# Attention with forget decay and a gated FFN on one core: last tokens' units earlier, turns of the second batch moved, PSUM slots of a pair swapped

**Chip, cores, metric.** One core of one Trainium2 chip. Times are device microseconds (us) of that core; quoted times are medians over runs. Every run named here was correct, and every profiled run was fast, with a granted TensorE clock of 0.998 to 1.000.

## The reference, cut

```python
# q, k, v: (B=8, H=8, S=576, D=64); f: (8, 8, 576); all float32
scores = scale * np.matmul(q, k.transpose(0, 1, 3, 2))
cum    = np.cumsum(np.log(np.clip(f, 0.0001, 1.0)), axis=-1)
scores = np.where(causal, -1e9, scores + cum[..., :, None] - cum[..., None, :])
attn   = softmax(scores)                       # cut
x      = (attn @ v).transpose(0, 2, 1, 3).reshape(4608, 512)
gate   = 1.0 / (1.0 + np.exp(-(x @ w_gate)))   # w_gate, w_val: (512, 1536)
out    = (gate * (x @ w_val)) @ w_out          # w_out: (1536, 512)
```

The output has 4608 tokens of 512 values in float32.

## The kernel before

The kernel interleaves two things on TensorE. The FFN runs in chunks of 512 tokens ("c0", "c1", ...), each of 36 steps; the step numbers below count through the chunks (step 46 is step 10 of c1). The attention of the batches that come later is put between the steps as small pieces of work. All 5259 matmuls of the trace write one PSUM tile, `ps`, which the kernel lays out as eight banks of 512 float32 per partition: banks 4 to 7 belong to the FFN, banks 0 and 1 are attention's slot 0, banks 2 and 3 its slot 1.

```python
def T_step(p, bank, copy_q, copy_k):        # a "turn": q and k of a head pair, transposed
    if bank < 4:
        slot_free(bank // 2)
    ...
    banks = [psh[:, 1024 * x:1024 * x + S] for x in (bank, bank + 1)]
    for t in range(TPP):
        for half, bank in zip((LO, HI), banks):
            for h in range(2):
                nc.tensor.transpose(...)    # 36 small transposes
    qT, kT = pair_T(p)
    for dst, bank, copy in ((qT, banks[0], copy_q), (kT, banks[1], copy_k)):
        copy(...)                           # on ScalarE (ACTC) or VectorE (DVEC)

def slot_free(slot):                        # let the chain run on until it lets go of the slot
    while chain and slot in chain_holds[0]:
        pop_chain()

def S_unit(p, u, slot, tag=None):           # a score unit: C, A, B, D (or Z: the last tokens)
    slot_free(slot)
    sc = 2 * slot
    ...                                     # matmuls of two heads into banks sc and sc + 1
    nc.scalar.activation(e[:, :, 0:w], ps[:, sc:sc + 2, 0:w], ACTF.Exp, scale=scale)
    ...                                     # causal mask on GpSimd

def out_two(p, now):                        # two pairs: sums, values, then a chain of VectorE work
    while chain:
        pop_chain()
    ...                                     # 120 matmuls; the values of pair p end in banks 2 and 3
    def last():                             # the last readers of banks 2 and 3
        for x, k, y in ((0, 2, 0), (0, 2, 1), (1, 1, 1)):
            part(x, k, y)                   # -> scaled(): tensor_tensor on VectorE, line 271
        cross_x(p, 2)
    both, beta = {0, 1}, {1}
    chain_holds[0] = both
    chain.extend([(flip, both), (lambda: spr(1), both), (lambda: part(1, 1, 0), beta),
                  (lambda: spr(0), beta), (last, set())])
    pop_chain(now)

def rest_turn():                            # last 64 tokens of batch 0, transposed into xR
    slot_free(1)
    ...                                     # 16 transposes of xt into banks 3 and 2 (line 435)
    ...                                     # 2 copies on ScalarE, 2 on VectorE (line 440)
```

The schedule of the second batch (batch 1), in c0, and of batches 2 and 3:

```python
for x, (w, bank, copy) in enumerate(((4, 0, DVEC), (4, 2, DVEC), (22, 0, ACTC), (24, 2, DVEC))):
    put(w, lambda p=P + x, bank=bank, copy=copy: T_step(p, bank, ACTC, copy))
for w, x, tag in ((7, 0, "D"), (9, 1, "A"), (11, 2, "B")):
    put(w, lambda p=x + 1, tag=tag: S_unit(p, "Z", 1, tag))
put(12, rest_values)
put(17, rest_turn)
batch(1, (6, 8, 10, 12, 13, 14, 15, 16, 24, 25, 26, 26, 27, 27, 28, 29), (18, 30),   # outs at 18, 30
      (0, 0, 0, 0, 1, 0, 1, 0, 0, 0, 1, 0, 1, 0, 1, 0))                             # slots
...
for b, ts in ((2, (36, 37, 39, 44)), (3, (67, 69, 71, 76))):
    for x, t in enumerate(ts):
        put(t, lambda b=b, x=x: T_step(b * P + x, (0, 2, 2, 2)[x], DVEC if x > 1 else ACTC, DVEC))
batch(2, (38, 40, 42, 43, 46, 47, 48, 49, 55, 57, 58, 59, 60, 61, 62, 62), (52, 64))
batch(3, (70, 72, 74, 75, 78, 79, 80, 81, 87, 89, 91, 92, 94, 95, 97, 98), (84, 100))
```

The softmax here doesn't subtract the row's maximum and nothing guards it: scores larger than these inputs give would overflow.

Of the kernel before, what the change touches and what calls it, by code (L numbers as in the profile page):

```python
# [15 lines left out]
def kernel(  # L16
# [12 lines left out]
    B, H, S, D = q.shape  # L29
# [142 lines left out]
    def pair_T(p):  # L172
        b, a = divmod(p, HPAIR)
        return qTs[b % 2][:, a, :], kTs[b % 2][:, a * SPAD:(a + 1) * SPAD]


    def k_at(p, jt):
        b, a = divmod(p, HPAIR)
        o = a * SPAD + jt * NP if b < 4 else (jt * HPAIR + a) * NP
        return kTs[b % 2][:, o:o + NP]  # L180
# [5 lines left out]
    def T_step(p, bank, copy_q, copy_k):  # L186
        if bank < 4:
            slot_free(bank // 2)
        b, hf, ho = half_of(p)
        src = qktiles[b, hf]  # L190
# [4 lines that stand above are left out]
                    nc.tensor.transpose(  # L195
                        bank[64 * h:64 * h + 64, t * QP:(t + 1) * QP],
                        src[half, ho + h, t * D:(t + 1) * D], ident_bf[half, half])
        qT, kT = pair_T(p)
        for dst, bank, copy in ((qT, banks[0], copy_q), (kT, banks[1], copy_k)):
            copy(dst[:, 0:S].rearrange("p (n t) -> p n t", t=TPP),  # L200
                 bank.rearrange("p (t n) -> p n t", t=TPP))
# [27 lines left out]
    def slot_free(slot):  # L229
        while chain and slot in chain_holds[0]:  # L230
            pop_chain()

    def S_unit(p, u, slot, tag=None):
        slot_free(slot)
        sc = 2 * slot
        qT = pair_T(p)[0]
        pieces, w, diag = UNITS[u]
        for jt, i0, i1, c in pieces:
            for h in range(2):
                hp = slice(64 * h, 64 * h + 64)  # L240
                nc.tensor.matmul(ps[:, sc + h, c:c + i1 - i0],  # L241
                                 k_at(p, jt)[hp, :], qT[hp, i0:i1],
                                 start=True, stop=True)
        tag = tag or TAGS.get(u, u)
        e = st[p, u] = esb.tile([128, 2, WIDE[tag]], BF16, tag="e" + tag, name="e" + tag)
        nc.scalar.activation(e[:, :, 0:w], ps[:, sc:sc + 2, 0:w], ACTF.Exp, scale=scale)  # L246
        m, pat = diag(e)
        nc.gpsimd.affine_select(out=m, in_=m, compare_op=ALU.is_ge, fill=0.0,  # L248
                                base=0, pattern=pat, channel_multiplier=-1)

    def vg_step(p, eng=None):
        b, a = divmod(p, HPAIR)
        vg = asb.tile([128, NJT, 2, D + 2], BF16, tag="vg", name="vg")
        st[p, "vg"] = vg
        if p < HPAIR:
            (eng or nc.gpsimd).tensor_copy(vg[:, :, :, D], g_bf[:, :, 2 * p:2 * p + 2])
        (eng or nc.gpsimd).tensor_tensor(  # L257
            out=vg[:, :, :, 0:D], in0=vbs[b % 2][:, :, 2 * a:2 * a + 2, :],
            in1=g_bf[:, :, 2 * p:2 * p + 2].unsqueeze(3).to_broadcast([128, NJT, 2, D]),
            op=ALU.mult)  # L260
# [111 lines left out]
    def out_two(p, now):  # L372
        while chain:
            pop_chain()
        Z = norm_tile("Z", [128, S])
        r = norm_tile("r", [128, 2, NB])
        R = norm_tile("R", [128, 2, S])
        for i, hi, o in main_tail(0):
            sums_two(p, o, i, hi)
        sums_of(Z, main_tail(0))  # L380
        for y in range(2):
            for x in (1, 0):
                i, hi, o = main_tail(2 - x)[y]
                vals_two(p + x, o, i, hi)

        def flip():
            inverse(r[:, 0, :], Z)
            nc.vector.tensor_copy(r[:, 1, :], r[:, 0, :])

        def spr(x):  # L390
            to_pair(r, x)
            spread(R[:, x, :], r[:, x, :])

        def part(x, k, y):
            i, hi, o = main_tail(k)[y]
            scaled(p + x, o, R[:, x, :], i, hi)

        def last():
            for x, k, y in ((0, 2, 0), (0, 2, 1), (1, 1, 1)):
                part(x, k, y)  # L400
# [7 lines that stand above are left out]
# [136 lines left out]
    DVEC, ACTC = nc.vector.tensor_copy, nc.scalar.copy  # L544
    T_step(0, 4, ACTC, DVEC)
    gps = ps[:, 7, 0:NJT * BH].rearrange("p (t n) -> p t n", t=NJT)
    for t in range(NJT):
        w = NP if t < NJT - 1 else TAIL
# [46 lines left out]
    def put(s, fn):  # L595
        at.setdefault(s, []).append(fn)

    def batch(b, units, outs, slots=(0, 0, 1, 0, 1, 0, 1, 0)):
        P = b * HPAIR
        for n, s in enumerate(units):  # L600
            p, u = P + n // 4, "CABD"[n % 4]

            def unit(p=p, u=u, n=n):
                S_unit(p, u, slots[n % len(slots)])
                if u == "C" and p not in late_vg:
                    vg_step(p)

            put(s, unit)
        for n, s in enumerate(outs):
            put(s, lambda n=n, now=3 if s % 36 < 2 * NFT else 4: out_two(P + 2 * n, now))  # L610
# [12 lines left out]
        return units, outs  # L623

    P = HPAIR
    for x, (w, bank, copy) in enumerate(((4, 0, DVEC), (4, 2, DVEC), (22, 0, ACTC), (24, 2, DVEC))):
        put(w, lambda p=P + x, bank=bank, copy=copy: T_step(p, bank, ACTC, copy))
    for w, x, tag in ((7, 0, "D"), (9, 1, "A"), (11, 2, "B")):
        put(w, lambda p=x + 1, tag=tag: S_unit(p, "Z", 1, tag))
    put(12, rest_values)  # L630
    put(17, rest_turn)
    batch(1, (6, 8, 10, 12, 13, 14, 15, 16, 24, 25, 26, 26, 27, 27, 28, 29), (18, 30),
          (0, 0, 0, 0, 1, 0, 1, 0, 0, 0, 1, 0, 1, 0, 1, 0))
    for p, w in zip(late_vg, (13, 15)):
# [9 lines left out]
    for b, ts in ((2, (36, 37, 39, 44)), (3, (67, 69, 71, 76))):  # L644
        for x, t in enumerate(ts):
            put(t, lambda b=b, x=x: T_step(b * P + x, (0, 2, 2, 2)[x], DVEC if x > 1 else ACTC, DVEC))
    batch(2, (38, 40, 42, 43, 46, 47, 48, 49, 55, 57, 58, 59, 60, 61, 62, 62), (52, 64))
    batch(3, (70, 72, 74, 75, 78, 79, 80, 81, 87, 89, 91, 92, 94, 95, 97, 98), (84, 100))
    o, G = 100, 99
    for b in range(4, B):  # L650
        units, outs = later(o, G)
# [59 lines left out]
```

## Time and profile before

| what | value |
|---|---|
| time | 376.23 us, median of 3 runs (375.75 to 376.54) |
| span in the profiled run | 375.7 us |
| TensorE busy | 96% of the span, and 91% of the chain that ended last |
| largest wait of TensorE after the first loads | 1.1 us (at 11.7 us, a score unit for a copy on ScalarE); past 28 us, where the change lies, 0.4 us apart from the stops named below |

The profiled run itself took 377.45 us, 1.2 us above the median. Single runs of one kernel differ by about 1 us here. There were also three stops of TensorE of which the profile can name no releaser ("issue"):

```profile
PE ps L352 <- issue: 0.8, 1, 0.8
```

(List of waits of TensorE, kernel before: line waited at, then us in total, times, longest us. This one is at 256.9 us; the second is at 222.6 us.) The third lies in the stretch that the change touches. In the chain of waits (start, length) it is the last line here, in the FFN work behind the 120 matmuls of `out_two` at step 18:

```profile
45.56 2.21 PE ps L352 x120
47.77 0.97 PE ps L455 x7
48.74 0.09 issue
```

### The profile page before, as it was taken

Reading aid. Unit: us, or ns where it says so; the run is one execution under the profiler, and the core shown is the slowest. Engines: PE = TensorE matmul, PEld = TensorE weight load, DVE = VectorE, ACT = ScalarE, POOL = GpSimd, SP = SyncE. Lnnn points to the kernel's source line nnn. Section 1 sums busy time; section 2 is a strip of 40 time slices with the busy share of each in tenths; the row PEclk is TensorE's granted clock in tenths of the full one; section 3 lists DMA queues with packets and bytes.
Section 4 is the critical chain, followed back from the end, with each engine's and each line's share of the span. In section 5 each row is a group of like instructions: output and inputs, shape, how many; then the busy total and the mean of one; then the engine's idle time right before and its main releaser. Section 6 shows DMA issues by size and latency. Waiting matters only on the chain.

```text
span 375.7 us, 12208 instructions
## 1 busy us (share of the span) xinstructions
PE 360.1 (96%) x5259; PEld 193.7 (52%) x5264; DVE 177.5 (47%) x382; ACT 196.4 (52%) x294; POOL 168.1 (45%) x265
## 2 busy tenths in 40 slices
PE   2889999999999999999999999999999999999996
PEld 1547544456655645454675545544456544444442
DVE  5874481566475565274708370747055713312320
ACT  5868745564836472847374727481647314323321
POOL 8896835064836664559665937460415000000000
PEclk9999999999999999999999999999999999999999
DMA  8999999599898986799984996687313131011002
GB/s 156 232 206 249 198 185 219 157 203 173 133 181 213 114 110 67 159 163 155 146 181 106 182 179 127 156 135 102 103 58 75 31 101 58 3 56 58 0 21 92
DMA packets 101349, 49.24 MB, mean 131 GB/s; under 512 B 72000, under 2 KB 94400, under 8 KB 101296
## 3 DMA queue, kind: packets, MB, share of 16 engines
q0 software_dynamic: 48704, 20.65, 44.1%
q1 hardware_dynamic: 52448, 27.68, 30.5%
q8 instruction: 41, 0.67, 0.8%
q10 hardware_dynamic: 144, 0.13, 0.1%
q14 instruction: 12, 0.10, 0.1%
HBM read 37.90 MB, written 9.44 MB: 126 GB/s over the span
## 4 chain that ended last, share of the span: by engine, by line
PE 91%; ACT 2%; DVE 2%; issue 2%; DMA 1%; POOL 1%; ACTq 0%; POOLq 0%
PE ps L455 49%; PE ps L495 17%; PE ps L352 8%; PE ps L504 8%; PE ps L241 6%; PE ps L300 1%; PE ps L195 1%; DMA qk_in<-in_k_dram 1%; DVE gv L465 1%; ACT eC L246 1%; DVE kT L200 1%; ACT eB L246 0%; DVE qT L200 0%; ACT sg L464 0%; POOL vg L257 0%
## 5 line engine op out<-in xcount | busy, mean ns | idle before, releaser
L455 PE MATMUL ps<-xR,w 64*128 64x512 bf16 x1728 | 205.7, 376 | 0.2
L465 DVE SCALAR_TENSOR_TENSOR gv<-sg,ps 128x512 bf16<-128x512 bf16 x108 | 74.0, 686 | 154.3 <-ACT sg L464 149.9
L455 PEld LDWEIGHTS <-w 64*128 64x128 bf16 x1728 | 88.6, 94 | 83.3 <-issue 3.6
L464 ACT ACTIVATE sg<-ps 128x512 bf16<-128x512 f32 x108 | 64.5, 598 | 86.9 <-PE ps L455 84.8
L248 POOL TENSOR_SCALAR_AFFINE_SELECT eC<-eC 128x256 bf16<-128x256 bf16 x32 | 13.0, 407 | 91.0 <-ACT eC L246 90.8
L241 PE MATMUL ps<-qT,kT 64*128 64x320 bf16 (+6 forms) x416 | 49.9, 275 | 2.9 <-ACT kT L200 1.3
L246 ACT ACTIVATE eC<-ps 128x896 bf16<-128x896 f32 (+1 forms) x32 | 28.1, 878 | 21.0 <-PE ps L241 21.0
L257 POOL TENSOR_TENSOR vg<-vb,g_bf 128x640 bf16<-128x640 f32 x30 | 37.9, 1263 | 0.0
L241 PEld LDWEIGHTS <-kT 64*128 64x128 bf16 x416 | 24.1, 96 | 23.7 <-issue 5.8
L482 ACT ACTIVATE ob<-ps 128x512 f32<-128x512 f32 x35 | 19.6, 596 | 32.1 <-PE ps L504 20.2
L495 PE MATMUL ps<-wox,gvx 64*128 64x512 bf16 x288 | 35.5, 376 | 0.0
L246 ACT ACTIVATE eA<-ps 128x896 bf16<-128x896 f32 (+2 forms) x33 | 30.4, 924 | 9.4 <-PE ps L241 8.7
L495 PE MATMUL ps<-wo,gv 64*128 64x512 bf16 x288 | 34.7, 376 | 0.4 <-issue 0.4
L504 PE MATMUL ps<-wo,gv 128*128 128x512 bf16 x140 | 32.3, 380 | 0.3 <-issue 0.2
L246 ACT ACTIVATE eB<-ps 128x768 bf16<-128x768 f32 (+2 forms) x33 | 27.5, 833 | 8.8 <-PE ps L241 7.4
L271 DVE TENSOR_TENSOR xR<-ps,R 128x64 bf16<-128x64 f32 (+2 forms) x68 | 26.2, 428 | 2.1
L108 POOL DMA_DIRECT2D vb<-in_v_dram x30 | 25.2, 849 | 0.2 <-issue 0.2
L263 DVE STREAM_TRANSPOSE R<-r 128x576 f32<-128x576 f32 (+1 forms) x32 | 24.6, 770 | 1.1
L495 PEld LDWEIGHTS <-gv 64*128 64x128 bf16 x288 | 15.4, 94 | 14.5 <-issue 1.3
L246 ACT ACTIVATE eD<-ps 128x640 bf16<-128x640 f32 x30 | 21.0, 701 | 3.0 <-PE ps L241 3.0
L495 PEld LDWEIGHTS <-gvx 64*128 64x128 bf16 x288 | 15.3, 94 | 13.2
L504 PEld LDWEIGHTS <-gv 128*128 128x128 bf16 x144 | 13.4, 98 | 16.8 <-issue 1.6
(82 smaller groups left out, 325.1 us busy)
## 6 DMA issues: line engine op xcount, KB each, us to landing
out_dram<-ob SPq DMA_DIRECT2D x35, 256.0 KB, 2.2
vb<-in_v_dram POOLq DMA_DIRECT2D x20, 256.0 KB, 5.4
xR<-xR SPq DMA_DIRECT2D x20, 144.0 KB, 3.4
gvx<-gv SPq DMA_DIRECT2D x12, 192.0 KB, 4.3
vb<-in_v_dram SPq DMA_DIRECT2D x8, 256.0 KB, 4.6
k_rows<-in_k_dram POOLq DMA_DIRECT2D x16, 128.0 KB, 6.8
q_rows<-in_q_dram POOLq DMA_DIRECT2D x16, 128.0 KB, 5.1
qk_in<-in_q_dram POOLq DMA_DIRECT2D x7, 288.0 KB, 6.7
```

The lines of the kernel that those rows point to most:

```text
L108: eng.dma_start(vbs[b % 2][0:n, t, h0:h1, :], rows)
L241: nc.tensor.matmul(ps[:, sc + h, c:c + i1 - i0], k_at(p, jt)[hp, :], qT[hp, i0:i1], start=True, stop=True)
L246: nc.scalar.activation(e[:, :, 0:w], ps[:, sc:sc + 2, 0:w], ACTF.Exp, scale=scale)
L257: (eng or nc.gpsimd).tensor_tensor(out=vg[:, :, :, 0:D], in0=vbs[b % 2][:, :, 2 * a:2 * a + 2, :], in1=g_bf[:, :, 2 * p:2 * p + 2].unsquee ...
L263: nc.vector.transpose(R.rearrange("p (n c) -> p n c", c=32), r.unsqueeze(2).to_broadcast([128, r.shape[1], 32]))
L271: nc.vector.tensor_tensor(out=xR[:, a, r0:r0 + n], in0=psf[:, o + i:o + i + n], in1=R[:, i:i + n], op=ALU.mult)
L352: nc.tensor.matmul(psf[32 * qd:32 * qd + 32, o + a:o + z], lhsT_of(jt, qd), e_of(u, qd)[:, c:c + z - a], start=(y == 0), stop=(y == len(to ...
L455: nc.tensor.matmul(ps[:, bk, :], w1[half, head, ft * NP:(ft + 1) * NP], xR[half, sl, t0:t0 + TCH], start=(first and x == 0), stop=(last an ...
L464: nc.scalar.activation(sg, ps[:, fb, :], ACTF.Tanh, scale=0.5)
L465: nc.vector.scalar_tensor_tensor(out=gv[:, ft, :], in0=sg, scalar=1.0, in1=ps[:, fb + 1, :], op0=ALU.add, op1=ALU.mult)
L495: nc.tensor.matmul(ps[:, bk, :], lhsT, rhs, start=(x == 0 and ft == 0), stop=(x == 1 and ft == NFT - 1))
L504: nc.tensor.matmul(ps[:, 4 + tt, :], gv[:, ft, tt * NP:(tt + 1) * NP], wo[:, ft, :], start=(ft == 0), stop=(ft == NFT - 1))
```

## The change

The intent is to fill TensorE's waits better. The units of the last tokens (Z) come three steps sooner so that their product needn't wait; the second turn of batch 1 leaves step 4, the third leaves step 22 for 17, takes slot 1 in place of slot 0 and has its k copy on VectorE, and the last tokens' turn (`rest_turn`) goes from 17 to 23. In batches 2 and 3 the second head pair takes its slots in the other order, and two units of batch 2 come a step later. (Some unchanged lines are left out of the diff.)

```diff
@@ -623,12 +623,12 @@
     P = HPAIR
-    for x, (w, bank, copy) in enumerate(((4, 0, DVEC), (4, 2, DVEC), (22, 0, ACTC), (24, 2, DVEC))):
+    for w, x, tag in ((4, 0, "D"), (6, 1, "A"), (8, 2, "B")):
+        put(w, lambda p=x + 1, tag=tag: S_unit(p, "Z", 1, tag))
+    for x, (w, bank, copy) in enumerate(((4, 0, DVEC), (10, 2, DVEC), (17, 2, DVEC), (24, 2, DVEC))):
         put(w, lambda p=P + x, bank=bank, copy=copy: T_step(p, bank, ACTC, copy))
-    for w, x, tag in ((7, 0, "D"), (9, 1, "A"), (11, 2, "B")):
-        put(w, lambda p=x + 1, tag=tag: S_unit(p, "Z", 1, tag))
     put(12, rest_values)
-    put(17, rest_turn)
+    put(23, rest_turn)
     batch(1, (6, 8, 10, 12, 13, 14, 15, 16, 24, 25, 26, 26, 27, 27, 28, 29), (18, 30),
           (0, 0, 0, 0, 1, 0, 1, 0, 0, 0, 1, 0, 1, 0, 1, 0))
@@ -644,8 +644,9 @@
-    batch(2, (38, 40, 42, 43, 46, 47, 48, 49, 55, 57, 58, 59, 60, 61, 62, 62), (52, 64))
-    batch(3, (70, 72, 74, 75, 78, 79, 80, 81, 87, 89, 91, 92, 94, 95, 97, 98), (84, 100))
+    MIXED = (0, 0, 1, 0, 0, 1, 0, 1, 0, 0, 1, 0, 1, 0, 1, 0)
+    batch(2, (38, 40, 42, 43, 46, 47, 48, 49, 55, 57, 59, 60, 60, 61, 62, 62), (52, 64), MIXED)
+    batch(3, (70, 72, 74, 75, 78, 79, 80, 81, 87, 89, 91, 92, 94, 95, 97, 98), (84, 100), MIXED)
```

## The prediction

> **What bounds the kernel now.** I read the page first, then the list of who TensorE waits for, then the chain of waits and the timelines of the steps that the change touches.
>
> ```profile
> span 375.7 us, 12208 instructions
> PE 360.1 (96%) x5259; PEld 193.7 (52%) x5264; DVE 177.5 (47%) x382; ACT 196.4 (52%) x294; POOL 168.1 (45%) x265
> PE 91%; ACT 2%; DVE 2%; issue 2%; DMA 1%; POOL 1%; ACTq 0%; POOLq 0%
> ```
>
> TensorE is busy for 96% of the span, and the chain that ended last is 91% TensorE. The change removes no matmul, copy or transfer: it moves work between steps and swaps PSUM slots. It can win only TensorE's stalls, and only those in the steps it touches (28 to 145 us). Matmul ends are modelled and hide short stalls, so I took start-to-start distances: a pair of 64-row, 512-column matmuls follows the last after 0.216 us, and what exceeds such a value is a stall. The real stalls in that stretch, in us: 0.28 at 30.12, 0.15 to 0.24 at 38.16, 0.11 at 40.03, 0.26 at 48.83, 0.56 at 56.14, 0.3 at 59.3, 0.33 at 65.5, 0.46 at 82.53, 0.31 to 0.44 at 96.57, 0.14 at 101.26, 0.45 at 121.20: about 3.5 us, 0.9% of the time. That is the ceiling of any gain, and already below 2%.
>
> The largest that the change aims at are the two waits of the score unit C for a copy on VectorE, in batches 2 and 3. In the list of TensorE's waits and then in the chain (start, length):
>
> ```profile
> PE ps L241 <- DVE kT L200: 0.6, 2, 0.3
> ...
> 78.90 0.88 PE ps L455 x8
> ...
> 79.83 0.61 ACT sg L464
> ...
> 80.46 0.69 DVE gv L465
> 81.14 0.67 DVE qT L200
> 81.81 0.67 DVE kT L200
> ...
> 82.53 0.35 PE ps L241
> ```
>
> At step 44 a turn of q and k (T_step) writes PSUM banks 2 and 3. VectorE has to do its gate product first, then both copies, until 82.48. The C unit of step 46 has slot 1, the same banks 2 and 3: its first matmul starts at 81.87, its second only at 82.53. A view of waits shows 0.3 of it; from starts, the step's FFN matmuls begin at 82.53 where 82.06 would do.
>
> [...]
>
> **The change, part by part.**
>
> *Slots in batches 2 and 3.* The second pair's C, A, B, D go from slots 1, 0, 1, 0 to 0, 1, 0, 1. C of step 46 then needs only slot 0, whose last reader, the exp of D at step 43, ended at 79.7. A of step 47 takes slot 1; it would start at 82.06 + 0.86 = 82.92, after the copies end at 82.48. B needs the exp of C as before, D that of A as before. So 82.53 - 82.06 = 0.47 us goes. In batch 3 (C of step 78) the FFN step starts at 121.21 where 120.77 would do: 0.44 us. Sum: **-0.91 us**. Both lie on TensorE's path, and nothing behind them has slack to swallow it except as below.
>
> *B and D of batch 2 one step later (58 to 59, 59 to 60).* B at 96.57 waits for the last normalisation, which reads banks 2 and 3 and ends at 96.5. A step later it finds them free: 0.3 to 0.4 us less there. But look at ScalarE:
>
> ```profile
> 97.24 0.81 ACT L246 ACTIVATE eB<-ps 128x768 bf16<-128x768 f32 x1
> 98.25 0.70 ACT L246 ACTIVATE eD<-ps 128x640 bf16<-128x640 f32 x1 [0.20 <-PE ps L241]
> 98.99 0.60 ACT L464 ACTIVATE sg<-ps 128x512 bf16<-128x512 f32 x1
> 99.49 0.91 ACT L246 ACTIVATE eC<-ps 128x896 bf16<-128x896 f32 x1
> 100.29 0.92 ACT L246 ACTIVATE eA<-ps 128x896 bf16<-128x896 f32 x1
> 101.34 0.81 ACT L246 ACTIVATE eB<-ps 128x768 bf16<-128x768 f32 x1
> 102.04 0.70 ACT L246 ACTIVATE eD<-ps 128x640 bf16<-128x640 f32 x1
> ```
>
> From the exp of B to that of the last D these seven take 0.81+0.70+0.60+0.91+0.92+0.81+0.70 = 5.45 of the 5.50 us between 97.24 and 102.74. ScalarE is full, and B's exp would start at 96.25 + 0.86 + 0.2 = 97.3, no sooner than now. TensorE saves at 58 and then waits at 61 (A for the exp of D, estimate 0.27) and 62 (D for the exp of A, 0.45). Net **-0.05 us**.
>
> *The first batch's last tokens (Z) from steps 7, 9, 11 to 4, 6, 8; the second turn of batch 1 from 4 to 10.*
>
> ```profile
> 28.87 0.83 PE L195 MATMUL ps<-ident_bf,qk_in 64*64 64x64 bf16 x72
> 29.39 1.28 DVE L465 SCALAR_TENSOR_TENSOR gv<-sg,ps 128x512 bf16<-128x512 bf16 x2 [2.58 <-PE ps L195]
> 29.63 0.89 PE L455 MATMUL ps<-xR,w 64*128 64x512 bf16 x3
> ...
> 38.16 0.51 PE L417 MATMUL ps<-vg,eD 128*64 128x65 bf16 x20
> ...
> 39.56 0.42 DVE L425 TENSOR_TENSOR gvx<-ps,r 128x256 bf16<-128x256 f32 x1
> ...
> 40.03 0.37 PE L241 MATMUL ps<-qT,kT 64*128 64x448 bf16 x2
> ```
>
> Two turns now fill 28.87 to 29.63; the FFN's second matmul then stands until 30.125 for the first gate product of VectorE, which ends at 30.08. One turn was thus free: it lay in time that TensorE had to wait anyway. With one Z unit (0.15 us) and one turn (0.38), TensorE comes to the same wait at 29.40 and waits longer. The turn that is now at step 10 costs its 0.41 us in full, the Z unit no longer at 7 gives 0.15 back: **+0.26 us**.
> What Z wins: the product of the last tokens with the values (38.16) waits some 0.24 us for the exp of the third Z, and that goes. But C of step 13 waits behind it for the normalisation on VectorE, which has the gate product of step 11 ahead of it. From the end of step 11: sigmoid +0.75, gate product +1.47, reciprocal +1.6, product +2.03. TensorE without the first stall gets there at 0.76 + 0.14 + 0.89 = +1.79 and waits 0.3 us; now both waits are 0.24 + 0.11 = 0.35. Net **-0.06 us**.
>
> *Third turn from 22 to 17, turn of the last tokens from 17 to 23.* The same matmuls (0.41 and 0.26 us) change places. What ScalarE does in 24 to 30 sets the stalls at 56.14 and 59.3: sigmoid of step 23, q copy of the fourth turn, exp of C, then A in the same slot. The sigmoid waits for TensorE now (0.70 us idle at 54.14), so emptying ScalarE before it wins nothing; the fourth turn may wait 0.1 to 0.2 us for the copies of step 23, behind which the sigmoid still runs. The data for the third turn lands before 43.97 (the next transfer of its queue), by the queue's rate of 512 KB in 2.6 us at about 41.5 (estimate); it is used at 44. **0.0 us**.
>
> Sum: -0.91 - 0.05 + 0.26 - 0.06 = -0.76 us, 376.23 - 0.76 = **375.5 us**.
>
> **The rivals.**
> 1. *ScalarE gives back more.* In 40 to 62 us the exps come in close order (0.70 to 0.92 us each, one per step of about 1 us), and the turn moved to step 10 brings a q copy of 0.64 there. For it: the stalls at 56.14 and 59.3 are ScalarE's. Against it: its list of waits shows idle time before most sigmoids. It would make 376 to 376.5.
> 2. *The rearranged steps 17 to 30 win too*, if the two ScalarE copies of the old step 22 (52.26 to 53.44) are what delays the units of 24 to 29. Against it: the idle 0.70 us after them. It would make 374.5 to 375.
> 3. *A turn finds its q and k not landed*, or slot 1 not free at step 17, and TensorE stands for 1 to 2 us: 377 to 378. The landing estimate speaks against it by 2 us.
> 4. *Short stalls that no semaphore explains* (0.26 at 48.83, 0.33 at 65.5) move with the instructions: a few tenths either way.
>
> **Range and chances.** Runs of the kernel before spread over 0.8 us (375.75 to 376.54), the same as the gain. Rivals 1, 2 and 4 each give half a microsecond or so, hence 374.6 to 376.4. 2% is 7.5 us, twice all stalls there are to win; a loss of that size needs a wait that nothing in the trace shows. Faster 0.01, same 0.98, slower 0.01.
>
> **What would show it.** Right: no k-copy wait of C in the list of TensorE's waits, FFN matmuls of steps 46 and 78 starting 0.2 us after C; the FFN's wait at step 4 longer, by about 0.23; C of step 13 still standing for VectorE; waits at steps 61 and 62 in place of 58; 56.14 and 59.3 as now. Wrong: a new wait in steps 10 to 24, a missing stall at step 25, or gains of batches 2 and 3 that the FFN phases after 145 us give back.

What the trace of the kernel before shows: VectorE ran the gate product, the q copy and the k copy in this order (starts 80.46, 81.06 and 81.73), C's second matmul started at 82.53, 0.05 us after the k copy's end at 82.48, and the FFN matmuls behind it stood until 82.53 as well.

## The result, and the profile after

The changed kernel took 378.15 us (378.02 to 378.43, 4 runs), the kernel before 375.99 us (375.52 to 376.54, 4 runs) beside it: ratio 1.0058, interval 1.0040 to 1.0075. By the 2% verdict that is "same"; it lies outside the predicted range, on the slow side. A ratio here is the mean time of one kernel's fast runs over that of the other's of the same rounds, so it is not quite the ratio of the quoted medians.

```profile
span 376.5 us, 12211 instructions
PE 359.4 (95%) x5259; PEld 192.9 (51%) x5264; DVE 177.6 (47%) x383; ACT 195.2 (52%) x293; POOL 168.6 (45%) x265
PE 90%; ACT 2%; issue 2%; DVE 2%; POOL 2%; DMA 1%; POOLq 0%; ACTq 0%
```

These are, of the kernel after, the span, the busy times and the chain's shares. The matmuls are the same 5259, and TensorE's busy time is no longer: what was added is waiting. To place it I compared the end of each of the 108 sigmoids (one for each pair of FFN steps) in the two traces. Where the difference changes, time was lost or won:

| where (us in the trace before) | change of the difference, us | what is there |
|---|---|---|
| up to the first sigmoid (29.35) | +0.15 | start, varies from run to run |
| steps 4 to 11 (38.71) | +0.46 | second turn, Z units |
| step 17 (46.25) | +0.10 | third turn in place of `rest_turn` |
| steps 18, 19 (50.51) | +0.85 | a stop named "issue" |
| steps 22, 23 (54.74) | +1.15 | `rest_turn` |
| steps 46, 47 (85.37) | -0.57 | slots, batch 2 |
| steps 52, 53 (93.22) | -0.17 | behind it |
| steps 58, 59 (99.59), then 72.. (118.01) | -0.59, then +0.60 | units of batch 2 a step later |
| steps 78, 79 (124.05) | -0.52 | slots, batch 3 |
| steps 84, 85 (131.89) | -0.17 | behind it |
| 222.6 and 256.9 | -0.53, -0.14 | stops named "issue", outside the change |

The early half (the first hunk, steps 4 to 24) costs 2.56 us in these traces, the late half (the second hunk, steps 46 to 81) gives about 1.4 us. The two largest losses head the list of waits of TensorE in the kernel after, right behind the start-up; neither was there in the kernel before in this size:

```profile
PE ps L352 <- issue: 1.6, 2, 0.9
PE ps L435 <- DVE xR L271: 1.4, 1, 1.4
```

**The wait of `rest_turn`.** First the timeline of the kernel before around step 23 (start, length, engine, line, operation), then that of the kernel after:

```profile
52.92 0.94 DVE L271 TENSOR_TENSOR xR<-ps,R 128x512 bf16<-128x512 f32 x3
...
53.98 0.48 PE L195 MATMUL ps<-ident_bf,qk_in 64*64 64x64 bf16 x36
```

```profile
54.54 0.94 DVE L271 TENSOR_TENSOR xR<-ps,R 128x512 bf16<-128x512 f32 x3
55.53 0.32 PE L435 MATMUL ps<-ident_bf,gvx 64*64 64x64 bf16 x16 [1.45 <-DVE xR L271]
...
56.28 0.56 DVE L440 COPY xR<-ps 64x256 bf16<-64x256 bf16 x2 [0.81 <-ACT xR L440]
...
56.90 0.48 PE L195 MATMUL ps<-ident_bf,qk_in 64*64 64x64 bf16 x36
```

The three products of line 271 are `last` of the `out_two` of step 18. They read banks 2 and 3, which `rest_turn` writes. In the kernel before they end at 53.86, and the next writer of slot 1, the fourth turn, comes just behind at 53.98. In the kernel after `rest_turn` is the next writer; it comes a step too early and TensorE stands: 1.45 us in the view, 1.61 us by start distances. The +1.15 us of the table at steps 22 and 23 stands, the same, in all five traces of kernels with both moves and no padding (three of the kernel after, two of the early half alone). Then the fourth turn has to wait for the copies of `rest_turn` as well, which share banks 2 and 3: 0.24 us, from start distances.

**The stop.** The chain of waits of the kernel after runs through it, inside the matmuls of `out_two`:

```profile
46.33 2.10 PE ps L352 x107
48.43 0.94 issue
49.37 0.29 PE ps L352 x13
```

No semaphore was signalled to it near 49.37. By start distances the stop was 1.11 us; the one shown in the kernel before (ending at 48.83) was 0.26 us. The stop also holds back what releases `rest_turn`: VectorE's gate product of step 19 stands for the sigmoid behind it, so `last` ends 9.2 us after `out_two` begins, and 8.4 us in the kernel before. VectorE's timeline of the kernel after:

```profile
52.16 0.69 DVE L465 SCALAR_TENSOR_TENSOR gv<-sg,ps 128x512 bf16<-128x512 bf16 x1 [0.72 <-ACT sg L464]
```

Experiments below ask what the stop is.

**The slots.** TensorE's timeline from step 46 on. In the kernel before, behind the wait that the prediction shows:

```profile
83.41 0.44 PE L241 MATMUL ps<-qT,kT 64*128 64x256 bf16 x3
...
83.69 0.24 PE L241 MATMUL ps<-qT,kT 64*128 64x192 bf16 x1
...
84.46 0.33 PE L241 MATMUL ps<-qT,kT 64*128 64x320 bf16 x2
84.63 0.38 PE L455 MATMUL ps<-xR,w 64*128 64x512 bf16 x1
84.63 0.33 PE L241 MATMUL ps<-qT,kT 64*128 64x320 bf16 x2
```

and in the kernel after:

```profile
84.62 0.35 PE L241 MATMUL ps<-qT,kT 64*128 64x448 bf16 x2
84.81 1.03 PE L455 MATMUL ps<-xR,w 64*128 64x512 bf16 x8
85.68 0.35 PE L241 MATMUL ps<-qT,kT 64*128 64x256 bf16 x4
```

After, both matmuls of C start together at 84.62 and the FFN 0.19 us behind: the wait for the k copy is gone. Before, one head's matmul of C had started 0.66 us ahead of the other's, and the matmuls, which the kernel issues in pairs (LO and HI), stayed out of step from then on: the two heads of a unit start 0.17 us apart (84.46 and 84.63, then 85.49 and 85.66), with an FFN matmul between them (84.63), through steps 47 to 51. In the kernel after the four matmuls of a unit come together. This 0.17 us comes back at the next `out_two` (128*32 in the trace), that of steps 52 and 84.

### The profile page after: what moved, and what is told of

Same layout as the page of the kernel before. It is cut to its first block, busy times and chain, and to the rows that moved or that the text cites. A ratio compares the mean times of both kernels' runs of the same rounds, so it can differ in the third digit from the quotient of the medians.

```text
span 376.5 us, 12211 instructions
## 1 busy us (share of the span) xinstructions
PE 359.4 (95%) x5259; PEld 192.9 (51%) x5264; DVE 177.6 (47%) x383; ACT 195.2 (52%) x293; POOL 168.6 (45%) x265
## 4 chain that ended last, share of the span: by engine, by line
PE 90%; ACT 2%; issue 2%; DVE 2%; POOL 2%; DMA 1%; POOLq 0%; ACTq 0%
PE ps L455 49%; PE ps L495 16%; PE ps L352 8%; PE ps L504 8%; PE ps L241 6%; PE ps L195 2%; DMA qk_in<-in_k_dram 1%; PE ps L300 1%; DVE gv L465 1%; POOL vg L257 1%; ACT eB L246 1%; POOL qk_in L97 1%; ACT sg L464 1%; ACT eA L246 0%; ACT eD L246 0%
## 5 line engine op out<-in xcount | busy, mean ns | idle before, releaser
L455 PEld LDWEIGHTS <-w 64*128 64x128 bf16 x1728 | 86.7, 94 | 83.7 <-issue 2.1
L241 PE MATMUL ps<-qT,kT 64*128 64x320 bf16 (+6 forms) x416 | 46.5, 275 | 2.2 <-ACT kT L200 1.1
L241 PEld LDWEIGHTS <-kT 64*128 64x128 bf16 x416 | 22.2, 96 | 24.0 <-issue 5.7
```

The costliest lines, as they stand in the source:

```text
L241: nc.tensor.matmul(ps[:, sc + h, c:c + i1 - i0], k_at(p, jt)[hp, :], qT[hp, i0:i1], start=True, stop=True)
L455: nc.tensor.matmul(ps[:, bk, :], w1[half, head, ft * NP:(ft + 1) * NP], xR[half, sl, t0:t0 + TCH], start=(first and x == 0), stop=(last an ...
```

## The experiments

Twelve runs in three sessions, each with its own runs of the kernel before; session A ran on one chip, B and C on another.

| session | kernel | median us (range) | ratio to before (95%) |
|---|---|---|---|
| A | before | 376.06 (375.53 to 376.94) | |
| A | late_only | 374.57 (373.62 to 374.92) | 0.9955 (0.9940 to 0.9971) |
| A | early_only | 378.07 (377.83 to 379.12) | 1.0055 (1.0040 to 1.0071) |
| A | turn34 | 377.54 (376.62 to 379.35) | 1.0047 (1.0022 to 1.0072) |
| A | turns_back | 375.09 (374.22 to 376.54) | 0.9975 (0.9957 to 0.9993) |
| B | before | 376.49 (375.82 to 378.64) | |
| B | after_again | 377.16 (376.98 to 377.68) | 1.0019 (1.0008 to 1.0031) |
| B | pad_after | 377.31 (376.64 to 377.66) | 1.0020 (1.0008 to 1.0032) |
| B | pad_before | 376.04 (375.73 to 376.81) | 0.9990 (0.9978 to 1.0003) |
| B | late_pad | 375.17 (374.52 to 376.35) | 0.9968 (0.9954 to 0.9983) |
| C | before | 376.40 (375.07 to 376.76) | |
| C | rest23 | 375.81 (375.35 to 378.35) | 1.0003 (0.9979 to 1.0028) |
| C | mixed_only | 375.20 (374.65 to 377.12) | 0.9983 (0.9961 to 1.0005) |
| C | after_third | 377.54 (376.23 to 378.67) | 1.0037 (1.0017 to 1.0057) |
| C | early_again | 379.01 (378.00 to 381.11) | 1.0082 (1.0055 to 1.0109) |

The theory: the loss is `rest_turn` waiting for slot 1, plus the stop; the late half wins what was predicted. The rivals: the later FFN phases give the late half's gain back; the second turn at step 10 is the main loss; the stop is a chance event of two single traces and the loss lies elsewhere.

### Session A: the halves, and where `rest_turn` goes

**late_only**: the kernel before with the second hunk of the diff alone.

> The kernel before with only the later half of the change: the mixed slots in batches 2 and 3 and the two units of batch 2 one step later. Theory (the later half wins, the earlier half loses): 1.2 to 1.5 us faster than before, as the sigmoids of the two traces show (0.57 + 0.17 at batch 2, 0.52 + 0.17 at batch 3, minus 0.05 each). Rival (the later half gives its gain back further on): within 0.4 us of before.

Measured: 374.57 us, 1.5 us less than before. In the traces the difference against before goes down by 0.57 (step 46), 0.17, 0.52 (step 78) and 0.16 us, and the -0.59 and +0.60 of the later units cancel; after step 84 nothing that the change could have caused is given back. The late half is a gain, and the largest of any version run.

**early_only**: the first hunk alone.

```diff
 # from the kernel after
-    batch(2, (38, 40, 42, 43, 46, 47, 48, 49, 55, 57, 59, 60, 60, 61, 62, 62), (52, 64), MIXED)
-    batch(3, (70, 72, 74, 75, 78, 79, 80, 81, 87, 89, 91, 92, 94, 95, 97, 98), (84, 100), MIXED)
+    batch(2, (38, 40, 42, 43, 46, 47, 48, 49, 55, 57, 58, 59, 60, 61, 62, 62), (52, 64))
+    batch(3, (70, 72, 74, 75, 78, 79, 80, 81, 87, 89, 91, 92, 94, 95, 97, 98), (84, 100))
```

> The kernel after without the later half: only the steps 4 to 24 are changed. Theory: 2.5 to 3.6 us slower than before; the trace shows TensorE standing some 1.5 us at the turn of the last tokens in step 23 until the last normalisation on VectorE ends, a longer way to step 13 by 0.4 to 0.5, and perhaps the 1.1 us without a semaphore inside the first batch-wide output block. Rival (the two traces differ by chance outside these steps): less than 1.5 us slower.

Measured: 378.07 us, 2.0 us more than before. The loss of the change is in this half. Its trace shows the +0.46 us of steps 4 to 11 and a stop of 0.97 us at the same place as in the kernel after.

**turn34**: the kernel after, with the last tokens' turn ten steps later, at 34.

```diff
-    put(23, rest_turn)
+    put(34, rest_turn)
```

> The kernel after with the turn of the last tokens in step 34 instead of 23, when slot 1 has been given free for two steps. Theory (the turn waits for the normalisation that holds slot 1): the 1.45 us wait of the turn for VectorE is gone from the list of waits, and the kernel is 1.0 to 1.6 us faster than after. Rival (TensorE is ahead of the units' exps anyway and waits as long at step 25): within 0.4 us of after, with a longer wait for the exp of C.

Measured: 377.54 us, 1.5 us above before, which is no better than the whole change did. The hoped-for recovery failed. The trace says why. By the sigmoids, steps 22 and 23 are no longer lost (-0.78 us against before at this place, since the third turn has left step 22 and nothing came in its stead), but 1.78 us is lost before c1 begins. The waits only moved: the fourth turn at step 24 is now the first writer behind `last` and stands (0.48 and 0.23 us at this step), and at step 34 `rest_turn` meets the slot held again, by the `out_two` of step 30 (0.96 us by start distances, 0.79 in the view):

```profile
70.19 0.32 PE L435 MATMUL ps<-ident_bf,gvx 64*64 64x64 bf16 x16 [0.79 <-DVE xR L271]
```

The mechanism is the same at each of the two places: the first writer of slot 1 within about 8 us of an `out_two` waits for its `last`.

**turns_back**: the kernel after, with the third turn and `rest_turn` as before. What is left of the early half is the Z units and the second turn.

```diff
-    for x, (w, bank, copy) in enumerate(((4, 0, DVEC), (10, 2, DVEC), (17, 2, DVEC), (24, 2, DVEC))):
+    for x, (w, bank, copy) in enumerate(((4, 0, DVEC), (10, 2, DVEC), (22, 0, ACTC), (24, 2, DVEC))):
-    put(23, rest_turn)
+    put(17, rest_turn)
```

> The kernel after with the turn of the last tokens back in step 17 and the third turn of batch 1 back in step 22. Theory: no wait of the turn for the normalisation[...]: about 2.0 to 2.6 us faster than after, 0.5 to 1.0 us faster than before. Rival (the long stop without a semaphore at 49 us does not depend on where the instructions lie): 1.0 to 1.6 us faster than after, with the stop of 1.1 us still there.

Measured: 375.09 us, 0.5 us above late_only and some 1.0 us below before. So the second turn with the Z units costs about 0.5 us (trace: 0.46), and the rest of the early half's 2.0 us, about 1.5, comes with the two moves that are undone here. That refutes the rival that the second turn is the main loss. Its trace shows no wait of `rest_turn` and no stop at the place in question. No run moved the third turn alone.

### Session B: what the stop is

Counting TensorE's weight loads and matmuls in order of start, every stop without a releaser of 0.1 us or more past 28 us, in all 14 traces, lies at one of five places: 1471, 3519, 4287, 7100 and 8120, each to within three or so (a few records are missing from two traces). No kernel shows all five; rest23 and turns_back show none. From the first place the others are 8, 11, 22 and 26 times 256 away, to within seven. Those at 3519 (0.35 us in mixed_only, 0.12 in early_only) and at 4287 (0.20 in early_only) are seen only there. The page also lists a DMA queue of the kind "instruction":

```profile
q8 instruction: 41, 0.67, 0.7%
```

(Queues of the page of the kernel after: transfers, MB.) 0.67 MB in 41 transfers is 16 KB each. The 5259 matmuls and 5264 loads, 10,523 instructions, over 41 is 257 for each: an estimate from these counts alone, as the trace doesn't show whom the queue serves. The three stops of the kernel before and the first of the kernel after ended 2.2 to 3.0 us after such a transfer had begun (46.66 to 48.83, 219.61 to 222.57 and 254.15 to 256.91 before; 47.17 to 49.37 after). This is nearness in time; that TensorE waits for a transfer is not shown by any trace or run. What a run can ask is whether a stop belongs to a place in the stream, as the counts suggest, and not to the work there: then instructions put in front shift it to other work. I put 32 dummy transposes (64 instructions with their loads) in front of the first score units:

```diff
+    for n in range(32):
+        half, bank = ((LO, 6), (HI, 3))[n % 2]
+        o = 64 * (n // 2 % 2)
+        nc.tensor.transpose(psh[o:o + 64, 1024 * bank:1024 * bank + 64], ident_bf[half, half],
+                            ident_bf[half, half])
     for p in range(HPAIR):
         S_unit(p, "U", p % 2)
```

in the kernel after (pad_after), in before (pad_before) and in late_only (late_pad). **after_again** is the kernel after, unaltered.

> The changed kernel itself, unaltered, so that it stands on one chip beside the kernel before and the padded ones. Both theories: 378.0 to 378.4 us. What is asked of its profile: whether the stop of TensorE without a semaphore comes again at the same instruction of its stream (behind the 1469th weight load or matmul), some 0.5 to 1.1 us long.

Measured: 377.16 us, +0.7 us against before, where the first measurement had +2.2. The stop at 1471 is again large, 1.04 us.

> The changed kernel with 32 dummy transposes (64 TensorE instructions, some 0.35 us) put in at 8 us, where TensorE waits for a copy anyway. Every later instruction stands 64 places further on in the stream. Theory (the stops at places 1469, 7095 and 8117, which are 256 apart but for a remainder[...]): no stop at the old instruction inside the output block; the place counted from the start stays a multiple of 256 from the others and now lies 64 instructions earlier in the work, where the stream is thinner, so 0.8 to 1.8 us faster than the changed kernel. Rival (the stop belongs to the output block and its data): the stop stays at the same matmul of the output block, and the time stays within 0.4 us of the changed kernel.

> The kernel before with the same 32 dummy transposes. Theory: its stops at places 1469 (0.26 us), 7095 (0.5) and 8117 (0.9) go or shrink; 0.5 to 1.5 us faster than before. Rival: within 0.4 us of before.

> The kernel before with only the later half of the change and the dummy transposes: a try at a kernel that beats both. If the two effects add, 1.5 us (later half, as measured) and 0.5 to 1.5 us (padding) faster than before: 373.0 to 374.1 us. Rival[...]: as the later half alone, 374.6 us, or 0.3 slower for the dummies.

Measured: 377.31, 376.04 and 375.17 us; the gains of 0.5 to 1.8 us that were expected of the padding did not come. In all three the stops at 1471 and at 8120 are gone, and that at 7100 stayed at its count, though other work is there now; it grew to 0.81, 1.13 and 0.79 us (0.51 before). So the stop at 7100 does belong to a place of the stream and not to the work, for the other two this is not shown, and shifting the work past them doesn't pay as a whole. For the loss of the change, pad_after tells more. Its stop in `out_two` is gone, which by the sigmoids wins 1.06 us at steps 18 and 19 against after_again, and yet its time is no better. Of the win, 0.29 us is lost again at step 23 and 0.82 us at the stop at 7100, which is larger; the stop at 8120, gone as well, gives 0.52 us, and up to the first sigmoid, where single executions differ, 0.84 us is lost. Its list of waits of TensorE:

```profile
PE ps L435 <- DVE xR L271: 1.6, 1, 1.6
...
PE ps L455 <- issue: 0.6, 1, 0.6
```

The wait of `rest_turn` took up part of it (1.77 us by start distances in place of 1.61): `out_two` begins at 46.2 and `last` ends at 54.59, 8.4 us later, just as in the kernel before (45.49 to 53.86). With no large stop in the way, the end of `last` is set by VectorE's own chain, and TensorE, which gets there sooner, waits longer. A large stop delays both: from the start of `out_two` to the end of `last` it is 9.1 to 9.2 us in the three traces with a stop of 1 us, and 8.5 to 8.6 us in the three with one of 0.4 to 0.5 us.

### Session C: the moves one by one

**rest23**: late_only, with `rest_turn` at 23 (the third turn stays at 22).

```diff
-    put(17, rest_turn)
+    put(23, rest_turn)
```

> The later half of the change and, of the earlier half, only the turn of the last tokens in step 23; the third turn of batch 1 stays in step 22, the Z units and the second turn stay where they were. Theory (two separate costs: the wait for the normalisation that holds slot 1[...]): the turn waits 0.8 to 1.2 us for VectorE's normalisation, the stop at place 1471 of the stream falls in plain steps behind the output block and stays under 0.4 us; so 0.9 to 1.4 us slower than the later half alone, near the kernel before (375.5 to 376.2). Rival (the wait at step 23 is only a consequence of TensorE having been stopped before): under 0.4 us slower than the later half alone.

The trace shows the wait without the stop, in the timeline around step 23:

```profile
52.28 0.94 DVE L271 TENSOR_TENSOR xR<-ps,R 128x512 bf16<-128x512 f32 x3
53.27 0.32 PE L435 MATMUL ps<-ident_bf,gvx 64*64 64x64 bf16 x16 [1.10 <-DVE xR L271]
```

By start distances 1.26 us here and 0.24 us at the fourth turn; the sigmoids show -0.61 us at steps 16 to 19 (nothing turned at 17, and before's stop missing) and +1.32 us at 22, 23. No stop at 1471. The wait and the stop are two separate costs. In time it had 375.81 us, 0.6 us above mixed_only of the same session; its ratio of 1.0003 is above the 0.9955 of late_only in session A, but overlaps with mixed_only's. The direction is that of the theory, the size is shown by the trace alone.

**mixed_only**: late_only, with batch 2's two units at 58 and 59 as before.

```diff
-    batch(2, (38, 40, 42, 43, 46, 47, 48, 49, 55, 57, 59, 60, 60, 61, 62, 62), (52, 64), MIXED)
+    batch(2, (38, 40, 42, 43, 46, 47, 48, 49, 55, 57, 58, 59, 60, 61, 62, 62), (52, 64), MIXED)
```

> The later half of the change without its smaller part: the slots are mixed, the units B and D of batch 2 stay in steps 58 and 59. Theory (the shift by a step wins nothing, ScalarE is full there): the same time as the later half, 1.3 to 1.7 us faster than before. Rival (the shift matters): 0.3 to 0.6 us slower than the later half.

Measured: 375.20 us, ratio 0.9983, whose interval overlaps that of late_only in session A. The time doesn't separate the two. In the trace of late_only the units' later step wins 0.59 us at steps 58, 59 and loses 0.60 by the start of c2, in two waits for ScalarE. Net zero. The trace of mixed_only also loses 0.58 us before c2, but to a stop at 3519, so the two traces set side by side would wrongly show the later step as a gain of 0.59 us.

**after_third** and **early_again**: the kernel after and early_only once more, to see whether the halves add up.

> The changed kernel again, beside its halves on one chip, because the two measurements so far differ (2.15 and 0.7 us slower than before). If the halves add: 0.3 to 0.8 us slower than before. If they don't: 2 us slower, as its earlier half alone.

> The earlier half of the change alone, on the same chip as the whole and the later half's slots, to see whether the halves add: 2.0 to 2.6 us slower than before, and the whole 1.3 to 1.7 us faster than this one.

Measured: 377.54 and 379.01 us: the late half is worth 1.5 us on top of the early one too, as alone. Against before the whole change was +2.2, +0.7 and +1.1 us in its three sessions, and the early half +2.0 and +2.6. The stop at 1471 was 1.11, 1.04 and 0.41 us in the three profiled runs of the kernel after, 0.97 and 0.44 in those of the early half. Its size varies from run to run of the same kernel. The trace of mixed_only, whose stream up to this place is that of the kernel before, has it at 0.71 us where the kernel before had 0.26.

## Why the prediction was wrong, step by step

The prediction was 375.5 us, -0.76 us; the first measurement gave +2.2 us and the two repeats +0.7 and +1.1. The class "same", given 0.98, came true. The late half was right in its mechanism and came out better; the early half held the error, and the prediction's own sign of being wrong, "a new wait in steps 10 to 24", is what the trace showed.

- **The step that failed: "Third turn from 22 to 17, turn of the last tokens from 17 to 23 ... 0.0 us."** I asked what the moved copies do to ScalarE and whether the data has landed, and only for the third turn whether slot 1 is free (rival 3). I never asked it for `rest_turn`. Step 23 lies in the stretch in which `out_two` of step 18 holds slot 1, until VectorE's `last`. The answer stood in the trace of the kernel before: `last` ended at 53.86 and the fourth turn, a step later, started at 53.98, so a writer one step earlier must wait about a step. Its size in the table is +1.15 us: the new wait of 1.61 us and the 0.26 us of the transposes themselves, less the 0.5 us of the third turn that left step 22, make 1.37. The 0.2 us between the two fits the stop of the kernel before: it parted the two matmuls of a pair (starts 48.36 and 48.83), and the FFN matmuls were still out of step at the third turn of step 22: the last one before it started alone, at 51.43, where the pair before had started at 51.22, which cost the kernel before another 0.21 us there. In pad_before, where this stop is gone, 0.26 us is won at step 19 and 0.20 at step 23. The 0.24 us of the fourth turn don't show in the sum: the difference of the sigmoids moves by less than 0.08 us from step 23 to c1, as the next unit then waits less for the exp of C (0.29 us in the view, 0.42 before). With the +0.10 us at step 17 it is +1.25 us for a step predicted as zero. turns_back (undone: 375.09 us) and rest23 (done alone: a wait of 1.26 us) show it from both sides. The prediction's "the fourth turn may wait 0.1 to 0.2 us" named the wrong waiter, and turn34 shows that going later only meets the next `out_two`.
- **Rival 4, short stalls without a semaphore: "a few tenths either way."** The size was off: +0.85 us at steps 18 and 19 in the first pair of traces, +0.78 and +0.15 in the two repeats. That the stop at 7100 keeps its place in the instruction stream is shown by the padded kernels (0.81, 1.13 and 0.79 us, with other work there); the stops at 1471 and 8120 were gone in them. What TensorE waits for there is not shown: the four that were compared ended 2.2 to 3.0 us after a transfer of the instruction queue had begun, but no experiment changed those transfers. Why the same stop is 1.1 us in one run and 0.4 in another stays open. Its place in the work may play a part: `out_two`, 240 records of matmuls and loads, begins at record 1215 in the kernel before and at 1255 in the kernel after, so the count 1471 falls just behind it there and inside it here. That was only argued, and the runs do not settle it: inside it the six stops were 0.41 to 1.11 us, behind it 0.26, 0.34 and 0.71 us and twice none. The other stall that the prediction named here, 0.33 us at 65.5, is none: the trace lacks the record of a matmul there (two weight loads follow one another), which stands in its place in the traces of the twelve runs.
- **Second turn and Z: +0.26 - 0.06 = +0.20 us; measured +0.46.** The wait at step 4 grew as predicted, from 0.28 to 0.49 us:

```profile
30.27 1.04 PE L455 MATMUL ps<-xR,w 64*128 64x512 bf16 x8 [0.32 <-DVE gv L465]
```

  (timeline of the kernel after; the wait in brackets is that for VectorE's gate product). So the second turn was free in its old place. Three terms were mis-sized: a turn costs 0.50 us where I took 0.41, because its first transpose starts 0.30 us after the last FFN pair in place of 0.216 (64*128 to 64*64 in the trace; the entry into `out_two`, 128*32, took the same 0.30 at 45.49 in the kernel before); the product of the last tokens (38.16) had hardly waited for the third Z unit, its 0.36 us from start to start being 0.31 in the kernel after, where it waits for nothing; and C of step 13 still stands (0.26 us in place of 0.11) for VectorE's division, which waits for the sigmoid of step 11. turns_back against late_only has the sum in time: +0.5 us.
- **Slots: -0.91 us; trace -1.4, timed -1.5 (late_only).** The wait for the k copy is gone at both places (-0.57 and -0.52 us where 0.47 and 0.44 were worked out). The term left out is the 0.17 us after each, which goes with the pairs of matmuls out of step (84.46 and 84.63). In the trace C's second matmul and the FFN behind it stood until 82.53, as the prediction had it, but not all of the delay ended with the wait.
- **B and D a step later: -0.05 us; trace 0.** B's wait at 96.6 went, and waits for ScalarE came at 101.8 (0.18 us) and 103.4 (0.39 us) in the place and kind that was named, here the second:

```profile
103.37 0.31 PE L241 MATMUL ps<-qT,kT 64*128 64x320 bf16 x2 [0.23 <-ACT eA L246]
```

- **ScalarE as a bound (rival 1)**: not seen. The FFN phases give nothing back either.

Of the terms in the first traces, 1.25 (the two turns), 0.85 (the stop) and 0.26 (second turn and Z) against the slots' extra -0.5 and the 0.05 of B and D make 1.9 us, which lead from -0.76 to the trace's sum of the touched stretch, 2.56 - 1.43 = +1.1. That the first measurement showed another microsecond over this isn't explained by the traces; the repeats lie at or below the sum. The direction (slower, by 0.2 to 0.6%) held in all three sessions, the size between sessions stays open.

The late half alone beats both kernels: 374.57 us, 0.9955 of the time before.

## What to carry to other kernels

Before moving work into a shared PSUM slot, look up when the slot's last reader ends on its own engine: in this kernel VectorE's chain let go of slot 1 some 8.4 us after `out_two` began, and 9.2 us where TensorE had stopped for 1 us in between. Work that lay inside a wait was free here and cost its full duration, with its entry, where TensorE was busy (the second turn: inside the wait of step 4, which was 0.28 us with it and 0.49 us with a Z unit in its stead; 0.50 us at step 10). When a unit writes two banks, hand it a slot of which both banks come free together: here a late second bank cost 0.74 us (0.57 and 0.17) where the profile listed a wait of 0.3.
